# Retention into a routed mixture of experts: small gate loads on another queue, and the first pair's loads and transposes reordered

## The chip, the core and the metric

The kernel runs on one core of a Trainium2 chip. The metric is the device time of one execution in microseconds (us), the median of several runs. A core has five engines that matter here. TensorE (PE, with its weight loads shown as PEld) multiplies and transposes. VectorE (DVE) and ScalarE (ACT) copy and combine. GpSimd (POOL) does elementwise work, scatters rows, and starts some transfers. SyncE (SP) starts nearly all transfers. "SPq" or "ACTq" in a row is the time in which an engine issues a transfer.

## The reference

```python
for t in range(S):                       # retention; B=4, H=8, S=768, D=64
    state = gamma * state + outer(k[:, :, t], v[:, :, t])
    y[:, :, t] = scale * einsum('bhd,bhde->bhe', q[:, :, t], state)
x = y.transpose(0, 2, 1, 3).reshape(3072, 512)
logits = x @ w_gate                      # 8 experts
e_idx = argmax(logits, axis=1)
gate_w = softmax(logits)[arange, e_idx]
eom = sigmoid(x @ w_output_gate)
for e in range(8):                       # w1: 8 x 512 x 1024, w2: 8 x 1024 x 512
    ye = relu(x[e_idx == e] @ w1[e]) @ w2[e]
    out[e_idx == e] = gate_w * eom[:, e] * ye
```

All data are float32.

## The kernel before

The retention is done in chunks of 128 tokens: six chunks for each of four batch rows, 24 in all. Two batch rows run side by side, so that the chunks come in 12 pairs. The loop over pairs (variable `p`, lines 686 to 828) is written out by hand in the order in which each engine is to work; nothing is reordered afterwards. Chunk numbers `n0 = 2p` and `n1 = 2p + 1` are the two of a pair.

For one pair the steps on TensorE are, in this order: the part that comes from the running state (`inter`, L385), the products of keys and queries (`scores`, L393, into four PSUM banks `sp[0]` to `sp[3]`, chunk `n0` in banks 0 and 1), the transposes of finished tokens of an earlier pair (`tokens`, L522), of gate logits (`turn_logits`, L448) and of queries for a later pair (`turn_queries`, L353), then the products with the values (`values`, L411), the state's update (`state`, L418), the counts for the router, the transposes of the next pair's keys (`turn_keys`, L340), more queries, and the gate logits (`logits`, L437). VectorE masks the scores (L401), scales the outputs (L428) and does the routing. ScalarE copies every transposed tile from PSUM to SBUF: keys and queries by the helper of L336, tokens as rows by L529 in `rows_out`. GpSimd scales the values (`prep_v`, L330), writes the row numbers into each row (L531) and scatters rows by expert into a DRAM table, `srt` (L538). A bank of `sp` can be written again only when its last reader is done, so a copy of ScalarE can hold TensorE up.

Queries are loaded for two chunks at a time (`load_q`, 512 KB, two buffers). For the very first tiles each batch row has a buffer of the same two, `q0`, loaded and turned in halves: `first_queries(ch, o)` (L303) loads half `o`, and `turn_first` (L358) and `keep_first` transpose and copy it. Half 0 serves pair 0, half 1 serves pair 1. `load_q(0, 1)` and `load_q(1, 1)` go into the buffers of `q0` and so wait for both halves to be turned. Pair 1 turns these queries: `part_queries` on ScalarE copies them apart into `qr` (by L336), and `turn_queries` transposes them, row 0's between the scores and the values of pair 1, row 1's near its end. From pair 2 to pair 9 one batch row's queries for a later pair are turned in each pair (`ahead`).

Loads of keys and values go through SP in program order: keys have six buffers, values four. Each transfer from SP or ACT signals on one of eight counters, handed out in turn. A transfer that reuses a counter waits for the one that had it before; the listings below show these waits as `DMAHW0` to `DMAHW7`.

The gate tables `w_gate` and `w_output_gate` are loaded into `wg` by four transfers of 8 KB (L314), which the first `logits` needs, at the end of pair 0. GpSimd starts the loads of the decay tables `gn` and `ga`. Before the first transposes TensorE runs nine products with zeros (`warm_up`).

At the loop's end a first part of one expert is computed from rows read back from `srt` (`head_load`, L573, issued in pair 10 when all scatters so far have landed). Then eight experts follow, with nearly nothing but matmuls (L985, L1008).

Of the kernel before, what the change touches and what calls it, by code (L numbers as in the profile page):

```python
# [33 lines left out]
def retention_moe_kernel(  # L34
# [14 lines left out]
    nc = tc.nc  # L49
    P = 128  # L50
    HP = P // 2
    B, H, S, D = q.shape
    E, DM, DF = w1.shape
    NT = B * S
    NC = S // P
    NCH = B * NC
# [181 lines left out]
    with ExitStack() as actx:  # L238
# [14 lines left out]
        def rows(x):  # L253
            return slice(x * HP, x * HP + HP)
# [56 lines left out]
        nc.scalar.dma_start(gv, dec_v)  # L311
        for o in range(2):
            for x, w in ((0, w_gate), (E, w_ogate)):
                nc.scalar.dma_start(wg[rows(o), :, x:x + E],  # L314
                                    w[o * DM // 2:(o + 1) * DM // 2].rearrange("(g p) e -> p g e", p=HP))
        load_v(0)
# [6 lines left out]
        load_v(3)  # L323
        load_q(0, 1)
        load_q(1, 1)

# [5 lines left out]
        def blocks(bank):  # L332
            return bank.rearrange("p (g t) -> p g t", g=NG)
# [184 lines left out]

        def tokens(i):
            px = blocks(sp[i % 2])  # L520
            for g in range(NG):
                nc.tensor.transpose(px[:, g], yts[i][:, g], ident)  # L522
            pxs[i] = px
# [142 lines left out]
        for o in range(2):  # L666
# [3 lines left out]
                            dec_c.rearrange("b x -> (b x)").unsqueeze(0).broadcast_to([P, 2 * NC * NG]))  # L670
        warm_up(misc, 9)
        turn_first(0, 0, yp[0])
        keep_first(0, 0, yp[0], nc.vector)
        turn_keys(0, yp[1])
        keep_keys(0, yp[1])
        turn_first(1, 0, st.rearrange("p a x -> p (a x)"))
        keep_first(1, 0, st.rearrange("p a x -> p (a x)"), nc.vector)
# [8 lines left out]
        for p in range(NCH // 2):  # L686
# [6 lines left out]

            if n0 + 4 < NCH:
                load_k(n0 + 4)
                load_v(n0 + 4)
            if p > 0 and nxt // 2 + 1 < NQ:
                load_q(nxt % 2, nxt // 2 + 1)
            if n1 + 4 < NCH:
                load_k(n1 + 4)  # L700
                load_v(n1 + 4)
# [13 lines left out]

            if p == 0:
                for ch in range(2):
                    turn_first(ch, 1, sp[ch])
                    keep_first(ch, 1, sp[ch], nc.scalar)
            if p >= 2:  # L720
                for i in (n0 - 4, n0 - 3):
                    tokens(i)
                    rows_out(i)
                    if not last:
                        scatter(i)
            if grp:
                turn_logits(grp)
            if p == PICK_AT:
                by = rank_key(totals(n0), io8)
# [4 lines left out]
            if p == 1:  # L734
# [3 lines left out]
                for r in range(2):  # L738
                    part_queries(1, 1, r)
            if ahead:  # L740
                turn_queries(*ahead, 0, sp[0])
                keep_queries(*ahead, 0, sp[0])
            if p == 10:
# [30 lines left out]
            if grp:  # L774
                bank = sp[3 if last else 0]
                counts(grp, bank)
                add_counts(grp, nc.gpsimd)
                route2(grp, bank)
                gates(grp, bank[:, 6 * E:6 * E + 4])
            if n0 + 2 < NCH:  # L780
                turn_keys(n0 + 2, sp[2])
                keep_keys(n0 + 2, sp[2])
                turn_keys(n0 + 3, sp[3])
                keep_keys(n0 + 3, sp[3])
# [7 lines left out]
            if last:  # L792
                for i in (n0 - 2, n0 - 1):
                    tokens(i)
                run_head(12)
                rows_out(n0 - 2)
                scatter(n0 - 2)
# [50 lines left out]
        for i in grp:  # L848
            tokens(i)
            rows_out(i)  # L850
            scatter(i)
            run_head(6)
# [406 lines left out]
```

## Time and profile before

| | |
|---|---|
| median of 3 runs | 421.1 us (419.83 to 422.4) |
| the profiled execution | 421.54 us |
| its span, first to last instruction | 419.6 us |
| TensorE busy | 404.4 us, 96% of the span |
| GpSimd, VectorE, ScalarE busy | 257.3, 222.8, 185.3 us |
| mean granted TensorE clock | 0.987 of full speed |
| moved by DMA | 75.75 MB, mean 181 GB/s |

The profile shows one execution. A row of its timeline has a start, a duration, an engine, a line of the kernel, an operation with its output and input, and a count; square brackets give the idle time of that engine just before and what ended it. Matmul ends are modelled, so that a busy TensorE isn't always one at its peak. The chain is followed back from the last instruction: at each step to what released it.

### The profile page before, as it was taken

The numbers are of one execution on the slowest core, as the hardware profiler recorded it, in microseconds if no ns is written. First come the engines' busy times: TensorE is split into PE (matmuls) and PEld (weight loads), VectorE is DVE, ScalarE is ACT, GpSimd is POOL, SyncE is SP. The second block draws the span as 40 slices with busy tenths as digits, with TensorE's granted clock in tenths as the row PEclk, the third lists the DMA queues.
The fourth block names the chain that finished last, engine by engine and source line by source line (L and its number), as shares of the span: only waits on it lengthen the run. The fifth ranks groups of instructions, "written<-read, shape, count | busy, mean of one in ns | idle before, by whom it ended". The sixth has DMA issues, their size and how long they took to land.

```text
span 419.6 us, 10492 instructions
## 1 busy us (share of the span) xinstructions
PE 404.4 (96%) x3611; PEld 378.3 (90%) x3611; DVE 222.8 (53%) x557; ACT 185.3 (44%) x360; POOL 257.3 (61%) x306
## 2 busy tenths in 40 slices
PE   7999999999999999999999999999999999999990
PEld 4878887888879999999999999999999999999880
DVE  3355667666687766744543553563555454553120
ACT  2366555555565325634533544443454454452110
POOL 3655664454587127883367777777786787876702
PEclk9899999999999999999999999999999999999996
DMA  8999788988744969797494588469459659620102
GB/s 187 256 240 244 214 232 220 252 204 220 203 141 154 248 147 269 222 211 191 141 224 140 148 200 207 155 180 232 136 172 237 176 168 208 214 75 28 47 3 75
DMA packets 130157, 75.75 MB, mean 181 GB/s; under 512 B 61748, under 2 KB 118216, under 8 KB 130064
## 3 DMA queue, kind: packets, MB, share of 16 engines
q1 hardware_dynamic: 122928, 59.38, 58.1%
q0 software_dynamic: 5904, 15.04, 10.3%
q8 instruction: 61, 1.00, 1.0%
q14 instruction: 32, 0.26, 0.2%
q10 hardware_dynamic: 1232, 0.06, 0.2%
HBM read 59.71 MB, written 15.30 MB: 179 GB/s over the span
## 4 chain that ended last, share of the span: by engine, by line
PE 79%; issue 5%; POOL 5%; DMA 5%; DVE 2%; ACT 1%; SPq 1%; POOLq 0%; ACTq 0%; DVEq 0%
PE h L985 29%; PE a L1008 27%; PE y L411 4%; PE s L393 4%; PE s L353 2%; PE st L418 2%; PE y L385 2%; POOL out_dram L215 2%; PE s L340 2%; PE s L522 1%; DMA qn<-in_q_dram 1%; PE s L622 1%; PE a L1036 1%; DMA raw<-in_moe_w_dram 1%; DMA srt<-row,pos 1%
## 5 line engine op out<-in xcount | busy, mean ns | idle before, releaser
L201 POOL TENSOR_TENSOR wlo<-raw,whi 128x512 fp32r<-128x512 f32 x56 | 74.9, 1338 | 44.3 <-ACT whi L193 27.1
L215 POOL DMA_INDIRECT out_dram<-ot,idi x85 | 84.7, 996 | 22.5 <-issue 17.7
L985 PE MATMUL h<-xh,whi 128*128 128x360 f32 (+5 forms) x256 | 84.3, 329 | 0.1
L985 PE MATMUL h<-xw,whi 128*128 128x360 f32 (+5 forms) x256 | 84.3, 329 | 0.0
L985 PE MATMUL h<-xh,wlo 128*128 128x360 f32 (+5 forms) x256 | 84.2, 329 | 0.0
L995 DVE SCALAR_TENSOR_TENSOR hl<-h,hh 128x192 fp32r<-128x192 f32 (+7 forms) x64 | 35.4, 554 | 82.8 <-ACT hh L994 81.2
L1008 PE MATMUL a<-hh,whi 128*128 128x392 f32 (+4 forms) x224 | 73.8, 329 | 0.0
L1008 PE MATMUL a<-hl,whi 128*128 128x392 f32 (+4 forms) x224 | 73.8, 329 | 0.0
L1008 PE MATMUL a<-hh,wlo 128*128 128x392 f32 (+4 forms) x224 | 73.5, 328 | 0.0
L994 ACT ACTIVATE hh<-h 128x192 fp32r<-128x192 f32 (+7 forms) x64 | 31.2, 488 | 73.5 <-PE h L985 73.5
L192 ACT CAST whi<-raw 128x512 fp32r<-128x512 f32 x64 | 39.6, 618 | 40.9 <-PE a L1008 31.1
L200 DVE TENSOR_TENSOR wlo<-raw,whi 128x512 fp32r<-128x512 f32 x60 | 42.4, 707 | 27.2 <-ACT whi L192 22.9
L985 PEld LDWEIGHTS h<-xh,whi 128*128 128x128 f32 x256 | 48.2, 188 | 0.9 <-issue 0.4
L985 PEld LDWEIGHTS h<-xw,whi 128*128 128x128 f32 x256 | 48.2, 188 | 0.6
L985 PEld LDWEIGHTS h<-xh,wlo 128*128 128x128 f32 x256 | 48.2, 188 | 0.2
L538 POOL DMA_INDIRECT srt<-row,pos x24 | 24.2, 1007 | 38.9 <-ACT row L529 31.2
L401 DVE TENSOR_TENSOR am<-s,mask 128x512 f32<-128x512 f32 x48 | 29.9, 684 | 30.6 <-PE s L393 28.5
L1008 PEld LDWEIGHTS a<-hl,whi 128*128 128x128 f32 x224 | 42.2, 188 | 0.3
L1008 PEld LDWEIGHTS a<-hh,wlo 128*128 128x128 f32 x224 | 42.2, 188 | 0.2
L1008 PEld LDWEIGHTS a<-hh,whi 128*128 128x128 f32 x224 | 42.2, 188 | 0.2
L193 ACT CAST whi<-raw 128x512 fp32r<-128x512 f32 x64 | 39.6, 618 | 1.1 <-DMA raw<-in_moe_w_dram 1.1
L927 ACT CAST xh<-xt 128x416 fp32r<-128x416 f32 (+2 forms) x28 | 15.1, 540 | 36.7 <-DVE xt L926 36.7
(201 smaller groups left out, 642.1 us busy)
## 6 DMA issues: line engine op xcount, KB each, us to landing
raw<-in_moe_w_dram SPq DMA_DIRECT2D x128, 128.0 KB, 4.8
raw<-in_moe_w_dram SPq DMA_DIRECT2D x64, 256.0 KB, 4.1
kn<-in_k_dram SPq DMA_DIRECT2D x24, 256.0 KB, 4.6
vn<-in_v_dram SPq DMA_DIRECT2D x24, 256.0 KB, 5.0
qn<-in_q_dram SPq DMA_DIRECT2D x10, 512.0 KB, 5.6
xl<-srt SPq DMA_DIRECT2D x12, 209.6 KB, 5.5
xl<-srt SPq DMA_DIRECT2D x8, 225.8 KB, 3.3
xl<-srt SPq DMA_DIRECT2D x8, 193.5 KB, 4.8
```

What stands on the lines that cost most here:

```text
L192: nc.scalar.copy(hi[:, 0], raw[:, 0])
L193: nc.scalar.copy(perm(hi), r2)
L200: (first or nc.vector).tensor_sub(lo[:, 0], raw[:, 0], hi[:, 0].bitcast(F32))
L201: (second or nc.gpsimd).tensor_sub(perm(lo), r2, perm(hi).bitcast(F32))
L215: st = nc.gpsimd.indirect_dma_start(out=dst, out_offset=bass.IndirectOffsetOnAxis(ap=idx, axis=0), in_=src, in_offset=None, bounds_check=n ...
L393: nc.tensor.matmul(sp[2 * (n % 2) + b][:, (2 * S_ + o) * P:(2 * S_ + o) * P + P], kt[n][rows(b), g], queries(n, g, b), start=True, stop=Tr ...
L401: nc.vector.tensor_tensor(out=a.rearrange("p s o t -> p (s o) t"), in0=sp[2 * (n % 2) + b].rearrange("p (x t) -> p x t", t=P), in1=mask.un ...
L538: s_ = nc.gpsimd.indirect_dma_start(out=srt, out_offset=bass.IndirectOffsetOnAxis(ap=rt.pop(("pos", i)), axis=0), in_=row.rearrange("p a x ...
L985: nc.tensor.matmul(ps[:, 0:C], l[:, 0, w], r[:, dc, 0:C], start=(n == 0), stop=(n == 3 * NDC - 1))
L994: nc.scalar.activation(hh, ps[:, 0:C], AF.Relu)
L995: nc.vector.scalar_tensor_tensor(out=hl, in0=ps[:, 0:C], scalar=0.0, in1=hh.bitcast(F32), op0=ALU.max, op1=ALU.subtract)
L1008: nc.tensor.matmul(accs[d][:, 0:C], l[:, 1, w], r[:, 0:C], start=(f == 0 and n == 0), stop=(f == NF - 1 and n == 2))
```

## The change

- The four loads of the gate tables move from ACT's queue to GpSimd's, behind `gn` and `ga`.
- Of the nine zero products seven stay ahead of the first transposes, and three come behind the first keys' transposes.
- The loads of row 0's and row 1's second queries (`load_q(0, 1)`, `load_q(1, 1)`) move into pair 0, each behind one of the loads of keys 4 and 5; the loads of values 4 and 5 come behind all of these.
- The second halves of the first queries are turned at the end of pair 0, behind the state's update, and not between its scores and values. Row 1's copy goes from ScalarE to VectorE.
- From pair 2 on the queries are turned first behind the scores, in bank 0; then the tokens of chunk `n0 - 4` in bank 1, the logits, and the tokens of chunk `n0 - 3` in bank 0. Both scatters come behind both `rows_out`.

```diff
-        for o in range(2):
-            for x, w in ((0, w_gate), (E, w_ogate)):
-                nc.scalar.dma_start(wg[rows(o), :, x:x + E], ...
...
-        load_q(0, 1)
-        load_q(1, 1)
...
-        def tokens(i):
-            px = blocks(sp[i % 2])
+        def tokens(i, bank):
+            px = blocks(bank)
...
-        warm_up(misc, 9)
+        for o in range(2):
+            for x, w in ((0, w_gate), (E, w_ogate)):
+                nc.gpsimd.dma_start(wg[rows(o), :, x:x + E], ...
+        warm_up(misc, 7)
         turn_first(0, 0, yp[0])
         keep_first(0, 0, yp[0], nc.vector)
         turn_keys(0, yp[1])
         keep_keys(0, yp[1])
+        warm_up(misc, 3)
         turn_first(1, 0, st.rearrange("p a x -> p (a x)"))
...
-            if n0 + 4 < NCH:
+            if p == 0:
+                load_k(n0 + 4)
+                load_q(0, 1)
+                load_k(n1 + 4)
+                load_q(1, 1)
+                load_v(n0 + 4)
+                load_v(n1 + 4)
+            elif n0 + 4 < NCH:
...
-            if p == 0:
-                for ch in range(2):
-                    turn_first(ch, 1, sp[ch])
-                    keep_first(ch, 1, sp[ch], nc.scalar)
+            if ahead:
+                turn_queries(*ahead, 0, sp[0])
+                keep_queries(*ahead, 0, sp[0])
             if p >= 2:
-                for i in (n0 - 4, n0 - 3):
-                    tokens(i)
-                    rows_out(i)
-                    if not last:
-                        scatter(i)
+                tokens(n0 - 4, sp[1])
+                rows_out(n0 - 4)
             if grp:
                 turn_logits(grp)
+            if p >= 2:
+                tokens(n0 - 3, sp[0])
+                rows_out(n0 - 3)
+                if not last:
+                    scatter(n0 - 4)
+                    scatter(n0 - 3)
...
-            if ahead:
-                turn_queries(*ahead, 0, sp[0])
-                keep_queries(*ahead, 0, sp[0])
...
+            if p == 0:
+                for ch in range(2):
+                    turn_first(ch, 1, sp[ch])
+                    keep_first(ch, 1, sp[ch], nc.vector if ch else nc.scalar)
             if n0 + 2 < NCH:
                 turn_keys(n0 + 2, sp[2])
```

First, SP's queue at the kernel's start, from its fourth transfer on (`kn` keys, `vn` values, `qn` queries; L303 loads a half of the first queries, L274 a whole tile; in brackets the engine or counter waited for). Before:

```order
L264 DMA kn<-in_k_dram 128x8x64 [waits DMAHW0_49]
L269 DMA vn<-in_v_dram 128x8x64 [waits DMAHW1_49]
L269 DMA vn<-in_v_dram 128x8x64 [waits DMAHW2_49]
L303 DMA qn<-in_q_dram 64x16x64 [waits DMAHW3_49]
L303 DMA qn<-in_q_dram 64x16x64 [waits DMAHW4_49]
L264 DMA kn<-in_k_dram 128x8x64 [waits DMAHW5_49]
L264 DMA kn<-in_k_dram 128x8x64 [waits DMAHW6_49]
L269 DMA vn<-in_v_dram 128x8x64 [waits DMAHW7_49]
L269 DMA vn<-in_v_dram 128x8x64 [waits DMAHW0_49]
L274 DMA qn<-in_q_dram 128x8x128 [waits DMAHW3_49,DMAHW1_49,PE_49]
L274 DMA qn<-in_q_dram 128x8x128 [waits DMAHW4_49,DMAHW2_49,PE_49]
L264 DMA kn<-in_k_dram 128x8x64
```

And now:

```order
L264 DMA kn<-in_k_dram 128x8x64
L269 DMA vn<-in_v_dram 128x8x64 x2
L303 DMA qn<-in_q_dram 64x16x64
L303 DMA qn<-in_q_dram 64x16x64 [waits DMAHW0_49]
L264 DMA kn<-in_k_dram 128x8x64 [waits DMAHW1_49]
L264 DMA kn<-in_k_dram 128x8x64 [waits DMAHW2_49]
L269 DMA vn<-in_v_dram 128x8x64 [waits DMAHW3_49]
L269 DMA vn<-in_v_dram 128x8x64 [waits DMAHW4_49]
L264 DMA kn<-in_k_dram 128x8x64 [waits DMAHW5_49]
L274 DMA qn<-in_q_dram 128x8x128 [waits DMAHW7_49,DMAHW6_49,PE_49]
L264 DMA kn<-in_k_dram 128x8x64
L274 DMA qn<-in_q_dram 128x8x128 [waits DMAHW0_49,PE_49]
```

Four early transfers have lost their wait for a counter, and the two large query loads stand one and two key loads later, still waiting for TensorE.

Second, TensorE in pair 0, from the last scores (`qt`, `kt` are turned queries and keys) to the next pair's keys. Before:

```order
L393 MATMUL s_127<-qt,kt 128x128
L358 MATMUL s_124<-ident,qn 128x64 x8
L358 MATMUL s_125<-ident,qn 128x64 x8
L411 MATMUL y_129<-am_246,vs 64x128 x4
L411 MATMUL y_130<-am_248,vs 64x128 x4
L411 MATMUL y_129<-am_258,vs 64x128 x4
L411 MATMUL y_130<-am_260,vs 64x128 x4
L418 MATMUL st<-vs,kn 64x64 x16
L340 MATMUL s_126<-ident,kn 128x128 x4
L340 MATMUL s_127<-ident,kn 128x128 x4
```

And now, with the lines of the changed file:

```order
L387 MATMUL s_127<-qt,kt 128x128
L405 MATMUL y_129<-am_247,vs 64x128 x4
L405 MATMUL y_130<-am_249,vs 64x128 x4
L405 MATMUL y_129<-am_259,vs 64x128 x4
L405 MATMUL y_130<-am_261,vs 64x128 x4
L412 MATMUL st<-vs,kn 64x64 x16
L352 MATMUL s_124<-ident,qn 128x64 x8
L352 MATMUL s_125<-ident,qn 128x64 x8
L334 MATMUL s_126<-ident,kn 128x128 x4
L334 MATMUL s_127<-ident,kn 128x128 x4
```

The sixteen half-query transposes moved from ahead of the values to behind the state's update.

Third, TensorE in pair 3, between scores and values (`s_124` and `s_125` are banks 0 and 1, `yt` tokens, `lt` logits, `qr` queries). Before:

```order
L393 MATMUL s_127<-qt,kt 128x128
L522 MATMUL s_124<-ident,yt 128x128 x4
L522 MATMUL s_125<-ident,yt 128x128 x4
L448 MATMUL misc<-ident,lt 128x128 x2
L353 MATMUL s_124<-ident,qr 128x128 x4
L411 MATMUL y_129<-am_733,vs 64x128 x4
```

And now:

```order
L387 MATMUL s_127<-qt,kt 128x128
L347 MATMUL s_124<-ident,qr 128x128 x4
L516 MATMUL s_125<-ident,yt 128x128 x4
L442 MATMUL misc<-ident,lt 128x128 x2
L516 MATMUL s_124<-ident,yt 128x128 x4
L405 MATMUL y_129<-am_734,vs 64x128 x4
```

The queries went from last to first, and the second use of bank 0 is now by tokens.

## Rows read from the trace of the kernel before

**Rows 1.** The page's chain that ended last, shares of the span.

```profile
PE 79%; issue 5%; POOL 5%; DMA 5%; DVE 2%; ACT 1%; SPq 1%; POOLq 0%; ACTq 0%; DVEq 0%
```

**Rows 2.** The chain, first 34 us: start, duration in us, what.

```profile
2.29 6.12 DMA qn<-in_q_dram
...
9.87 3.52 PE s L393 x32
...
14.24 0.68 PE s L358 x8
14.91 1.90 PE y L411 x32
...
20.37 1.99 PE s L393 x32
...
22.72 0.90 PE s L353 x8
...
33.01 1.10 PE s L522 x7
```

**Rows 3.** TensorE by windows: stretch, length, busy, granted clock, DMA share, GB/s.

```profile
5.00:9.20 4.20, 2.62 (x22) 1.00 1.21 240
9.20:12.60 3.40, 3.40 (x30) 0.55 1.11 244
```

**Rows 4.** Timeline of the first 35 us.

```profile
1.25 4.02 PE L167 MATMUL misc<-wz 128*128 128x512 bf16 x9 [1.25 <-DVE warm L90]
...
3.27 0.61 POOL L669 DMA_DIRECT2D ga<-in_dec_c_dram  x1
4.73 0.39 SPq L264 DMA_DIRECT2D kn<-in_k_dram  x1
8.45 0.71 PE L358 MATMUL st<-ident,qn 64*128 64x64 f32 x8 [1.58 <-DMA qn<-in_q_dram]
9.91 2.04 POOL L330 TENSOR_TENSOR vs<-vn,gv 128x512 f32<-128x512 f32 x2 [6.03 <-DMA vn<-in_v_dram]
14.65 2.23 SPq L274 DMA_DIRECT2D qn<-in_q_dram  x2
20.47 1.14 ACT L336 COPY qr<-qn 128x512 f32<-128x512 f32 x2 [0.70 <-DMA qn<-in_q_dram]
...
31.12 1.14 ACT L336 COPY qr<-qn 128x512 f32<-128x512 f32 x2 [0.69 <-DMA qn<-in_q_dram]
```

**Rows 5.** DMA from 2 to 30 us, all queues.

```profile
DMA packets 23585, 6.76 MB, mean 241 GB/s; under 512 B 20485, under 2 KB 23519, under 8 KB 23583
```

**Rows 6.** DMA from 2 to 8.4 us, ACT's queue: packets, MB, share.

```profile
q10 hardware_dynamic: 1232, 0.06, 12.1%
```

**Rows 7.** Timeline of pair 5, scores to values.

```profile
62.30 2.48 DVE L401 TENSOR_TENSOR am<-s,mask 128x512 f32<-128x512 f32 x4 [2.69 <-PE s L393]
...
63.09 1.21 PE L522 MATMUL s<-ident,yt 128*128 128x128 f32 x8
63.84 1.28 ACT L529 ACTIVATE row<-s,gate 128x512 f32<-128x512 f32 x2 [2.17 <-PE s L522]
...
64.59 0.42 PEld L353 LDWEIGHTS s<-ident,qr 128*128 128x128 f32 x4 [0.31 <-ACT row L529]
...
65.32 1.02 POOL L538 DMA_INDIRECT srt<-row,pos  x1 [3.69 <-ACT row L529]
...
66.82 0.98 POOL L538 DMA_INDIRECT srt<-row,pos  x1 [0.28 <-POOL row L531]
```

**Rows 8.** Waits from 30 to 125 us: total, times, longest.

```profile
PEld s L353 <- ACT row L529: 1.8, 6, 0.4
...
PEld y L411 <- POOL vs L330: 0.8, 1, 0.8
```

**Rows 9.** The chain in pairs 9 to 11.

```profile
105.51 4.82 DMA srt<-row,pos
...
116.52 1.03 POOL srt L538
```

More of the change, by code (lines that the diff above doesn't have):

```diff
@@ L311, in retention_moe_kernel @@
         nc.scalar.dma_start(gv, dec_v)
-        for o in range(2):
-            for x, w in ((0, w_gate), (E, w_ogate)):
-                nc.scalar.dma_start(wg[rows(o), :, x:x + E],
-                                    w[o * DM // 2:(o + 1) * DM // 2].rearrange("(g p) e -> p g e", p=HP))
         load_v(0)
@@ L670, in retention_moe_kernel @@
                             dec_c.rearrange("b x -> (b x)").unsqueeze(0).broadcast_to([P, 2 * NC * NG]))
-        warm_up(misc, 9)
+        for o in range(2):
+            for x, w in ((0, w_gate), (E, w_ogate)):
+                nc.gpsimd.dma_start(wg[rows(o), :, x:x + E],
+                                    w[o * DM // 2:(o + 1) * DM // 2].rearrange("(g p) e -> p g e", p=HP))
+        warm_up(misc, 7)
         turn_first(0, 0, yp[0])
@@ L692, in retention_moe_kernel @@
             last = p == NCH // 2 - 1
-            if n0 + 4 < NCH:
+            if p == 0:
[6 more added lines that the diff above has]
+            elif n0 + 4 < NCH:
                 load_k(n0 + 4)
                 load_v(n0 + 4)
-            if p > 0 and nxt // 2 + 1 < NQ:
-                load_q(nxt % 2, nxt // 2 + 1)
-            if n1 + 4 < NCH:
+                if nxt // 2 + 1 < NQ:
+                    load_q(nxt % 2, nxt // 2 + 1)
                 load_k(n1 + 4)
@@ L793, in retention_moe_kernel @@
                 for i in (n0 - 2, n0 - 1):
-                    tokens(i)
+                    tokens(i, sp[i % 2])
                 run_head(12)
@@ L848, in retention_moe_kernel @@
         for i in grp:
-            tokens(i)
+            tokens(i, sp[i % 2])
             rows_out(i)
```

## The prediction

> **What bounds the kernel now.** I read the chain of waits first, then the clock by windows, the timeline of the first 35 us, and the timeline of one middle pair. TensorE holds 79% of the chain [rows 1], and from the second half on it is nothing but matmuls that the change doesn't touch. What the change can move lies in the first 125 us: the start, where the chain goes through a load, and the waits between scores and values.
>
> At the start the chain is one load: the first half of row 1's queries, issued at 2.29 and landed at 8.41 [rows 2]. TensorE stands idle for 1.58 us until then [rows 4]. After that gap the granted clock falls: it is 1.00 from 5.0 to 9.2 and 0.55 from 9.2 to 12.6 [rows 3], that is mostly the lower level (1.2 GHz), in a stretch in which TensorE is busy throughout. The 32 score products of pair 0 take 3.52 us there, those of pair 1 take 1.99 [rows 2]. DMA is the second bound: 6.76 MB go from 2 to 30 us, 241 GB/s in the mean [rows 5], and twice ScalarE waits for queries of a later pair (at 20.47 and 31.12 [rows 4]).
>
> In a middle pair TensorE hardly waits. The one wait that the change aims at is 0.31 us, where the queries' transposes need bank 0 and ScalarE is still copying tokens out of it [rows 7]; all of these come to 1.8 us from 30 to 125 us [rows 8].
>
> **The change part by part, the start.** The gate loads: ACT's queue used 12.1% of the DMA engines from 2 to 8.4 us, 0.77 us [rows 6]. The four gate loads are 4 x 256 of its 1232 packets, so 0.64 us. GpSimd can begin them at 3.88 (3.27 + 0.61 [rows 4]), so part of them still goes ahead of row 1's queries. Bounds: 0 and 0.64 us earlier; I take 0.3.
>
> The Trainium skill, "DMA: Bandwidth & Descriptors", section "Issuing engines are not separate DMA queues", says that transfers started by ScalarE, SyncE or GpSimd run on the same 16 engines and interleave, so that another starter saves only the time of issuing. By it the 0.3 would be 0. No row here shows gate loads that GpSimd issues.
>
> GpSimd pays for them with its own time. The trace has no such issue on GpSimd; the nearest rows are 0.61 us for `ga` [rows 4] and 1.02 for a scatter [rows 7]. Four end between 6.3 and 8.0. GpSimd then waits for the values anyway, until 9.91 [rows 4], so I count nothing. The cover is gone from 1.5 us each on ((9.91 - 3.88) / 4).
>
> SP's earlier transfers: the fourth was held until 4.73 [rows 4], and is now free at once. The engines were at 240 GB/s from 5.0 to 9.2 [rows 3], against a mean of 241 [rows 5], so an earlier issue mostly lengthens the queue. I count it only as what keeps DMA from running dry.
>
> The zero products: nine took 4.02 us, 0.45 each [rows 4]. Seven free TensorE 0.9 us earlier, but the next thing it needs, row 1's queries, isn't there earlier by that. The three behind the first keys last up to 1.34 us and lie in the idle 1.58, so they cost nothing unless the queries land over 0.24 us earlier than now; at full clock they are shorter. They leave at most about 1.0 us of idle time where 1.58 stood. Whether the clock then holds isn't in any row. Bounds: 0 and 1.53 us (3.52 - 1.99); I take it that it holds, as TensorE's time between 5 and 9.2 is filled much better than before.
>
> Pair 0 by my choices: scores start at 9.57 and end at 11.56. VectorE masks bank by bank at 0.62 each (2.48 / 4 [rows 7]), from 10.6 to 13.15. The values' scaling is done at 11.95 (9.91 + 2.04 [rows 4]). The last quarter of the value products comes behind the last mask, a quarter of 1.90, and ends at 13.65, where it was 16.81 (14.91 + 1.90 [rows 2]). So 3.16 us are gained, but the half-query transposes, twice 0.68 [rows 2], which lay beside the masks, now stand by themselves behind the state: 1.8 left. They also put one more copy of ScalarE (0.57, half of 1.14 [rows 4]) ahead of the key copies. I take 0.3 us of that as visible: 1.5.
>
> What is late next is the load of row 0's second queries. It waits for both halves to be turned, it stands behind keys 4, and pair 1's query transposes at 22.72 [rows 2] need it. Before, it was issued at 14.65, landed at 20.47 [rows 4], and had 1.7 us of slack with a copy of 0.57. Keys 4 ahead of it cost 0.262 MB / 241 GB/s = 1.1 us. It can make up at most that by DMA that never runs dry. So it lands between 20.4 and 21.6, and the transposes come at 21.0 to 22.2: a gain of 0.5 to 1.7 us, whatever TensorE gained. A second cap stands behind: the next queries land at 31.12 [rows 4], with nothing removed ahead of them, are copied by 31.7, and are now wanted right behind pair 2's scores, where the tokens stood at 33.01 [rows 2]: 1.3 us. I take 1.1 for the whole start.
>
> **The change part by part, pairs 2 to 11.** In eight pairs the queries go first. TensorE's work between the two uses of bank 0 is the same: four transposes in between and the logits. The copy that has to be done in time is now that of the queries, 0.57, and no more that of the tokens, 0.64 (1.28 / 2 [rows 7]). So of each 0.31 us wait about 0.06 goes: 0.5 us in all. Bounds: 0, and the whole 1.8 plus pair 2.
>
> The first scatter of a pair comes 0.84 us behind the first tokens' copy (63.84 + 0.64, 65.32 [rows 7]). That copy is now 0.58 later, behind the queries'. Between the two scatters lay 0.48 us (65.32 + 1.02 to 66.82, of which 0.28 idle [rows 7]), 0.20 of it a copy that goes ahead. So the second ends 0.4 later. That hides in GpSimd's wait of 3.69 [rows 7], except in pair 9: there the chain runs through that scatter's landing [rows 9] into the read of sorted rows, and 0.4 us count. Pair 10's scatters, also on the chain [rows 9], get 0.2 back. In pairs 10 and 11 no queries are turned, and the tokens go first into bank 1, whose mask ends 0.62 later than bank 0's: nearly 0.5 us twice, against the 0.8 us in which TensorE waited for GpSimd there [rows 8] and the 0.5 gained before. It hides. Sum: -0.5 + 0.4 - 0.2 = -0.3.
>
> **Sum.** 1.1 + 0.3 = 1.4 us off. The profiled execution, 421.54 us with a span of 419.6, becomes 420.1; it lies 0.44 above the median, and on the median of 421.1 the same gives 419.7.
>
> **The rivals.**
> - Scores stay cold. For: nothing shows how little idle time the clock forgives, and seven zero products instead of nine open a new gap ahead of the first transposes. Then pair 0's scores take 3.52 from 9.57, masks end near 14.4, values at 14.9, and with 1.36 for the moved transposes and 0.3 for copies 0.25 us is left: 0.25 + 0.3 = 0.55 off, 420.5.
> - DMA doesn't bind. For: 241 GB/s is a mean with stretches in which SP was held. Then row 1's queries land 0.64 earlier, the start gains 1.5 + 0.3, and pairs 2 to 9 lose half of their waits, 0.9: 2.7 off, 418.4. Against: both caps.
> - Slower: the second queries come late. Their load now waits for transposes behind the state, not behind the scores. If the scores stay cold these end near 16.5, where they ended at 14.92 (14.24 + 0.68 [rows 2]), so the issue at 14.65 becomes 16.5 or more. With 5.8 us to landing and 1.1 for keys 4 they land at 22.3 to 23.4 and pair 1 stalls; row 1's, one key load further back, then hold ScalarE, which has pair 1's state to copy. It decides once they land after 22.15 (22.72 - 0.57), and costs 0.7 to 2.9 us: less 0.3, about 422.6.
> - GpSimd late. At twice a scatter's 1.02 us each, the four issues would end at 12.0, the values' scaling 2.1 us late, pair 0 about 1.5 worse than forecast: 421.2.
>
> The trace has GpSimd's issue of `ga` at 0.61 us [rows 4]. The Trainium skill, "SBUF — State Buffer", section "SBUF: two separate sides", warns that GpSimd can't write the descriptors of its transfers while VectorE runs certain operations, so that one which takes about 620 ns alone (section "A bandwidth-pool intuition that's wrong") takes about 3100. The trace agrees with the lower figure, and nothing here shows the higher; by that the four would end near 16.3, an estimate, and GpSimd would be late.
>
> **How the numbers follow.** Forecast 0.47, cold scores 0.22, DMA not binding 0.14, late queries 0.12, GpSimd late 0.05. The likeliest case alone spans 418.9 to 420.6. For 8 in 10 I go from 418.0, which holds most of the third case, to 422.3, half of the fourth. A change of 0.5%, 2.1 us, is about what a measurement of this kernel can tell from none: faster is below 419.0, slower above 423.2. Faster: most of the third case and a quarter of the forecast, 0.26. Slower: half of the late queries and the tail of GpSimd, 0.08. The rest, 0.66.
>
> **What would show it.** Right: a granted clock near 1.00 from 9 to 13 us, pair 0's scores in about 2 us, values ending near 13.7, pair 1's query transposes at 21 to 22 us with ScalarE waiting for the load just before, a 0.25 us wait in each middle pair, now ahead of tokens, and the first scatter 0.6 later within its pair. Wrong: scores at 3.5 us (cold), query copies landing after 22 us, GpSimd's value scaling starting later than 10 us, or a middle pair more than 0.2 us shorter, which would mean that the reordering is worth more than one copy's difference.

## The result: slower, by a stop in code that wasn't touched and by a longer end

The changed kernel takes 423.22 us (median of 22 runs, 421.0 to 427.53), the kernel before 420.48 on the same chip (22 runs, 419.42 to 424.0): ratio 1.0056, 95% interval 1.0038 to 1.0074. The ratio is that of the fast runs, without the one of 427.53 us. The forecast was 419.7 with a range up to 422.3. The profiled execution took 423.69 us, its span is 421.8.

Up to the main loop the profiled execution gains 0.44 us, where 1.4 was forecast. The chain of the kernel after, first 24 us (start, duration, what):

```profile
3.25 6.12 DMA kn<-in_k_dram
...
10.13 1.99 PE s L387 x32
...
13.35 1.16 PE y L405 x16
14.51 0.93 PE st L412 x32
...
16.24 5.37 DMA qn<-in_q_dram
...
21.62 0.63 ACT qr L330
...
22.30 1.18 PE s L347 x8
```

The scores take 1.99 us in place of 3.52 [rows 2], and the clock holds, where it was 0.55 [rows 3]. A window with no record of the clock reads 1.00; the record begins at 4.75 us here and at 6.11 in the kernel before, so the 1.00 of [rows 3] is a reading from 6.11 on only.

```profile
5.00:9.20 4.20, 2.27 (x21) 1.48 (x19) 0.69 (x1) 0.59 (x1) 1.34 (x3) 1.00 1.12 233
9.20:12.60 3.40, 3.17 (x46) 2.73 (x44) 1.97 (x4) 0.59 (x1) 2.19 (x3) 1.00 1.06 236
```

TensorE was busy for 2.27 us of the first window, less than before (2.62 [rows 3]). What it waited for next came no earlier: row 1's first queries let it go on at 8.61 (8.45 [rows 4]), the scores begin at 10.13 (9.87 [rows 2]), and the values' scaling begins at 10.39 (9.91 [rows 4]).

The next limit is the late load of the second queries: ScalarE waits for it, 3.02 us idle, where it waited 0.70 [rows 4]. GpSimd issues the gate tables in 0.65 us each and is then held by the load of the values, not by its own work:

```profile
3.85 0.65 POOL L667 DMA_DIRECT2D wg<-in_moe_w_gate_dram  x1
...
8.61 0.71 PE L352 MATMUL st<-ident,qn 64*128 64x64 f32 x8 [1.74 <-DMA qn<-in_q_dram]
...
10.39 2.05 POOL L324 TENSOR_TENSOR vs<-vn,gv 128x512 f32<-128x512 f32 x2 [4.05 <-DMA vn<-in_v_dram]
...
21.62 1.14 ACT L330 COPY qr<-qn 128x512 f32<-128x512 f32 x2 [3.02 <-DMA qn<-in_q_dram]
```

In the pairs the wait on bank 0 is smaller and has moved to the tokens (1.8 us before [rows 8]). The second row is the wait on bank 1 in pairs 10 and 11; the 0.8 us for GpSimd [rows 8] are gone. Waits from 30 to 125 us:

```profile
PEld s L516 <- ACT qt L330: 1.4, 8, 0.3
...
PEld s L516 <- DVE am L395: 1.3, 2, 0.7
```

In pair 5 the first scatter starts 3.56 us behind the first mask, where it was 3.02 (65.32 - 62.30 [rows 7]): 0.5 later, as forecast 0.6.

```profile
61.92 2.48 DVE L395 TENSOR_TENSOR am<-s,mask 128x512 f32<-128x512 f32 x4 [2.69 <-PE s L387]
...
65.48 1.03 POOL L532 DMA_INDIRECT srt<-row,pos  x1 [4.09 <-ACT row L523]
```

The loss lies behind all this. Stretches of the two profiled executions, in us, from the starts of the first matmul of each rank (ranks are the experts in the order of their size):

| stretch | before | after | |
|---|---|---|---|
| up to the main loop | 151.97 | 151.53 | -0.44 |
| ranks 1 to 4 | 125.93 | 125.88 | -0.05 |
| rank 5 | 34.06 | 35.46 | **+1.40** |
| ranks 6 to 8, to the last matmul's start | 97.39 | 97.18 | -0.21 |
| from there to the last scatter's start | 1.76 | 1.75 | -0.01 |
| last scatter's start to the end of the span | 8.47 | 10.03 | **+1.56** |

Rank 5 holds a stop in the middle of twelve matmuls that follow one another without a semaphore. The chain of the kernel after:

```profile
279.70 2.11 PE a L1016 x12
281.81 1.43 PE h L993 x8
283.23 1.27 issue
284.50 0.98 PE h L993 x4
```

"Issue" means that nothing in the profile held the engine. The instruction queues suggest what did, and the experiments below bear it out. The page of the kernel after:

```profile
q8 instruction: 61, 1.00, 1.0%
q14 instruction: 33, 0.27, 0.2%
```

Queue 8 brings 61 pieces of 16,384 bytes, queue 14 brings 33 of 8,192, while the kernel runs. Queue 8 is taken to be TensorE's program and queue 14 that of the other engines; the profile doesn't name them. A count of the built program, which no profile shows, puts the weight load ahead of the ninth matmul at instruction 8190 of TensorE, with 64 B each two short of the edge at 8192. The trace has the fetch of the next piece from 281.94 to 282.98, and the ninth matmul at 284.50, 2.56 us behind the fetch's start. So the stop is a sum: the fetch starts 0.29 us behind the step's first matmul, the code is usable 2.56 later, and eight matmuls of 0.178 us pass meanwhile: 0.29 + 2.56 - 1.42 = 1.43 late. (Of that the chain calls 1.27 "issue".) The kernel before has the same edge five matmuls later in its program (10 instructions: one warm-up product of two, eight added waits), its fetch starts at 282.04, and its matmuls are late by 0.14 only, from the 13th on (284.41).

The Trainium skill, "Advanced Engine Details and Errata", section "ISA Cache", says that a line of an engine's instruction memory is 16 KB, or 256 instructions. The trace agrees for the 61 pieces of queue 8 and not for the 33 of queue 14, which are of 8 KB. What a late line costs, the 2.56 us here, that section doesn't say.

The end is GpSimd's closing sequence, which the profile doesn't count as busy. From the packed trace, GpSimd alone (start and duration in us; `before_pool7` is explained below):

```
before          after           before_pool7
411.11 0.98     411.80 0.98      409.81 0.98   last scatter
413.34 0.02     414.87 0.02      412.42 0.02   wait
413.43 0.02     416.99 0.02      412.51 0.02   wait
  ... 3 more      ... 3 more       ... 3 more
414.31 0.04     417.35 0.04      413.18 0.04   wait
415.91 0.69     417.44 0.83      413.27 0.69   INC_SWDGE_SEM
416.63 2.12     418.30 2.69      414.00 2.12   DRAIN
```

Both kernels stand still once in it, before for 1.6 us ahead of the seventh instruction, after for 2.1 us ahead of the second. Counted from the beginning of GpSimd's program it is the same place, number 1043: the gate tables put five instructions more in front. Queue 14 starts a piece at 413.57 in the kernel before and at 414.37 in the kernel after, 2.34 and 2.62 us ahead of the end of the stop, much as on TensorE; in all 13 profiles with this stop it is 2.1 to 2.6. That the stop waits for this piece is argued: the profile doesn't name the engine, a piece starts then in the seven profiles without the stop too, and 1043 isn't a multiple of the 128 instructions that 8 KB would hold at 64 bytes. The drain is 0.57 us longer.

### The profile page after: what moved, and what is told of

Same layout as the page of the kernel before. It is cut to its first block, busy times and chain, and to the rows that moved or that the text cites. A ratio compares the mean times of both kernels' runs of the same rounds, so it can differ in the third digit from the quotient of the medians.

```text
span 421.8 us, 10498 instructions
## 1 busy us (share of the span) xinstructions
PE 402.2 (95%) x3612; PEld 375.9 (89%) x3612; DVE 223.9 (53%) x558; ACT 185.5 (44%) x359; POOL 260.0 (62%) x310
## 4 chain that ended last, share of the span: by engine, by line
PE 87%; issue 4%; DMA 3%; POOL 2%; DVE 1%; SPq 1%; ACT 0%; DVEq 0%; POOLq 0%
PE h L993 29%; PE a L1016 27%; PE y L405 5%; PE s L387 5%; PE s L516 3%; PE s L616 3%; PE y L596 2%; PE s L347 2%; PE y L379 2%; PE st L412 2%; PE s L334 2%; POOL out_dram L215 2%; DMA kn<-in_k_dram 1%; PE misc L431 1%; PE a L1044 1%
## 5 line engine op out<-in xcount | busy, mean ns | idle before, releaser
L201 POOL TENSOR_TENSOR wlo<-raw,whi 128x512 fp32r<-128x512 f32 x56 | 75.0, 1340 | 45.5 <-ACT whi L193 31.4
L1002 ACT ACTIVATE hh<-h 128x192 fp32r<-128x192 f32 (+7 forms) x64 | 31.3, 489 | 73.8 <-PE h L993 73.8
```

Of the source, the lines that this page charges most:

```text
L201: (second or nc.gpsimd).tensor_sub(perm(lo), r2, perm(hi).bitcast(F32))
L1002: nc.scalar.activation(hh, ps[:, 0:C], AF.Relu)
```

## The experiments

Theory A: what counts is where the code lies against the edges of its pieces, and how soon their fetch starts. Theory B: chance of one execution, or transfers that meet. Others are named where they came up. The runs were made on different chips. On two of them (the runs marked 430) the kernel before takes about 430 us, on the others 420 to 421; ratios are always to the kernel before on the same chip.

**TensorE's code.** First the changed kernel again:

> The changed kernel as it is, a second profile of it. Theory A (where the code lies): the main loop again starts near 151.7 us on TensorE (152.14 in the kernel before), TensorE again stands still 1.2 to 1.3 us in front of the ninth of twelve matmuls of the second step of expert rank 5, and from the last scatter's start to the span's end it is again about 10.0 us, so about 2.5 us over the kernel before. Theory B (accident of one execution, or transfers that meet): the stop is gone or stands at another place, the end is nearer 8.5 us, and the span nearer 419.5 us.

Measured (430): 437.78, ratio 1.0153 (1.0102 to 1.0203). The stop is there at the same matmul with the same 1.27 us, the end 9.5 us. As A had it, and not as B. But the main loop starts at 161.3 us, which neither had said (below).

The kernel before, its code moved by 10:

```diff
-        warm_up(misc, 9)
+        warm_up(misc, 8)
+        for _ in range(6):
+            nc.tensor.matmul(misc[:, 0:85], wz[:, 0:P], wz[:, 0:85], start=True, stop=True)
```

> The kernel before, with the last of its nine 512-column warm-up matmuls cut into six of 85 columns: five weight loads and five matmuls more, nearly the same columns, nothing else. TensorE's program behind them lies 10 instructions further on, as it does in the changed kernel. Theory A (where the code lies): the 1.27 us stop of the changed kernel appears here, before the ninth matmul of the second step of rank 5; span and time go up by 1.2 to 1.5 us, the end of the program (8.5 us from the last scatter) stays. Theory B (accident, or transfers that meet): no stop, within 0.3 us of the kernel before. Theory C (one of the three parts of the change itself costs it, through queue or semaphores): no stop either, since none of the three is in.

Measured (430): 1.0013 (0.9984 to 1.0041). A miss in size: the ninth matmul is late by 0.34 us, not by 1.4, and the time alone doesn't tell A from B or C. Its fetch started 1.05 us ahead of the step, in the changed kernel 0.29 behind the step's start; from fetch to use it is 2.81 and 2.56. So the place alone doesn't set the stop. It sets how much time the fetch has, and the fetch's start varies.

The changed kernel, its code moved by 246 more:

```diff
+        def pad(s, n, C):       # only in the arm for the largest size, which isn't taken
+            ...
+                nc.tensor.matmul(hps[s % 4][:, 0:C], hi[:, 0, 0:P], xs[e][0][:, 0, 0:C], ...)
...
+                if e == 1:
+                    first_mm.insert(0, lambda C: pad(s, 18 if f < 5 else 17, C))
```

> The changed kernel with 123 matmuls (246 instructions) in arms of the second expert rank's steps that the data don't take, so they are never executed; from rank 3 on TensorE's program lies 256 instructions behind where it lies in the kernel before, that is at the same place within a 16 KB piece (10 + 246 = 256 instructions of 64 B: the program's 15,018 were fetched in 61 pieces, 1.00 MB). Theory A (where the code lies): no stop in rank 5, the main loop 1.3 us shorter, span near 420.5 us, about 1.3 us under the changed kernel; the end of the program stays near 10 us, since GpSimd's program hasn't moved. Theories B and C: as the changed kernel within 0.3 us. Either could lose up to 2 us more where the longer unused arms are jumped over.

Measured (430): the stop is gone (late by 0.37), rank 5 takes 34.29 us, 1.17 less than in `after_again`. The time, 438.15, is no lower, where 1.3 us less was expected. The six runs of either kernel lie over 2 and 9 us apart, so their medians can't show it; the profiled execution, the longest of its six, also started its main loop 1.2 us later.

And moved by 8 the wrong way:

```diff
-        warm_up(misc, 7)
+        warm_up(misc, 6)
+        for _ in range(5):
+            nc.tensor.matmul(misc[:, 0:102], wz[:, 0:P], wz[:, 0:102], start=True, stop=True)
```

> The changed kernel with one of its first seven warm-up matmuls cut into five (8 instructions more, the same columns): the 16 KB edge in rank 5's second step falls before the fifth of its twelve matmuls in place of the ninth. Theory A: the stop stands there, 0.7 us longer than in the changed kernel if the fetch starts as early: 1.6 to 2.1 us; time 0.5 to 0.9 us over the changed kernel (1.004 to 1.0056 of the kernel before), so about 1.006 to 1.007. Theory B: the stop stays where and as long as it was, or goes.

Measured: 425.16, ratio 1.0098 (1.0068 to 1.0127). The stop is where A put it and 1.95 us long; the time is more than forecast, and the granted clock then falls to the lower level (0.51 for 3.4 us), which costs 1.04 us more. Chain and windows:

```profile
281.10 0.72 PE h L995 x4
281.81 1.95 issue
283.76 2.23 PE h L995 x8
285.99 3.15 PE a L1018 x12
```

```profile
281.00:284.60 3.60, 1.65 (x10) 1.33 (x9) 1.80 (x4) 1.14 (x2) 2.16 (x2) 1.00 1.12 195
284.60:288.00 3.40, 3.40 (x12) 3.40 (x11) 0.58 (x1) 0.51 (x1) 1.45 (x2) 0.51 1.18 226
288.00:292.00 4.00, 4.00 (x24) 4.00 (x24) 0.78 (x2) 1.65 (x3) 1.51 (x2) 0.99 0.62 153
```

The twelve second products take 3.15 us in place of 2.11. All profiles together, by the matmul of the step that the trace shows late (late: its start less the start of the one before, less 0.18; a step has twelve first and twelve second products):

| late matmul | late, us | kernels |
|---|---|---|
| 5 | 2.11 | after_pe8 |
| 9 | 1.43, 1.43, 1.15, 0.89, 0.89, 0.34 | after, after_again, after_gates_back, after_third, after_pool2, before_pe10 |
| 10 | 0.71 | only_mid |
| 13 | 0.56, 0.40, 0.28, 0.14, 0.14 | only_start_2, only_gates, only_start, before, before_2 |
| none | 0 | before_pool7 |
| 13 or 14, code moved by 256 | 0.14 to 0.43 (six) | after_pe256, after_both (2), realigned (2), mid_realigned |

**GpSimd's code and the gate tables.**

```diff
-            nc.gpsimd.iota(rows, ...)
+            for _ in range(3):          # in the overflow part, never executed
+                nc.gpsimd.iota(rows, ...)
```

> The changed kernel with two GpSimd instructions (one iota written three times) in the part that runs only when tokens overflow, which they don't here: never executed. GpSimd's closing instructions lie two further on, so that all of them begin behind the place at which both kernels waited for code (before its seventh closing instruction in the kernel before, before its second in the changed one: the same place in the program, counted from its beginning). Theory A: that wait, 2.1 us between the first two closing instructions of the changed kernel, goes, and the end comes 1.5 to 2 us earlier: 8 to 8.5 us from the last scatter; the 1.27 us stop of TensorE stays; time 1.5 to 2 us under the changed kernel. Theories B and C: the end stays near 10 us or moves without an order to it.

Measured (430): 7.95 us from the last scatter to the end, 1.6 less than in `after_again`; as A had it. The median, 437.14 against 437.78, is 0.64 lower and not 1.5 to 2, and with six runs each that shows nothing either way.

The gate tables alone on GpSimd, and the changed kernel with them back:

```diff
-                nc.scalar.dma_start(wg[rows(o), :, x:x + E], ...     # only_gates; after_gates_back
+                nc.gpsimd.dma_start(wg[rows(o), :, x:x + E], ...     # is the reverse on the kernel after
```

> The kernel before with the first part of the change alone: the four gate-table loads issued by GpSimd and no longer by ScalarE. GpSimd's program lies 5 instructions further on, TensorE's one. Theory E (the gate tables on GpSimd's queue are paid for at the end: GpSimd's closing drain took 2.69 us in all of the kernels with them there and 2.12 us in all without, and its closing instructions wait once more for code): from the last scatter to the end 9.5 to 10 us in place of 8.5, everything before it as in the kernel before; 1.0 to 1.5 us slower. Theory A alone (only where the code lies): 0.7 to 1 us slower, with the drain at 2.12 us. Theory F (the new start of the first pair is what costs most runs about 3 us, through the clock or the late query loads): as the kernel before within 0.5 us.

> The changed kernel with the four gate-table loads back on ScalarE's queue, in their old place. GpSimd's program lies where it lies in the kernel before; TensorE's 9 instructions further on. Theory E: closing drain 2.12 us, 8.5 us from the last scatter to the end, 1.2 to 1.5 us faster than the changed kernel; what is left over the kernel before is the stop of up to 1.4 us in rank 5 (theory A). Theory F: no faster than the changed kernel in the median, since the start is left as it is, though drain and end go back.

Measured: 1.0036 (1.0013 to 1.0058) and 1.0022 (0.9996 to 1.0048); ends of 9.52 and 8.42 us, drains of 2.69 and 2.12. Then the unchanged kernel with eight of those `iota` in place of one:

> The kernel before with seven GpSimd instructions in the overflow part that never run: its closing instructions lie just where they lie in the changed kernel with two more, which ended 7.8 to 8.0 us after the last scatter with a drain of 2.69 us. Theory A: 7.2 to 7.5 us from the last scatter to the end, drain 2.12 us; about 1.1 us faster than the kernel before. Theory E alone (the end depends on the gate tables, not on where the code lies): 8.4 to 8.7 us, as the kernel before.

Measured: 419.68, ratio 0.9971 (0.9947 to 0.9994), end 7.14 us; the listing above shows the 1.6 us wait gone. All profiles:

| closing code | gate tables by | profiles | end, us | drain |
|---|---|---|---|---|
| as before | ScalarE | 5 | 8.42 to 8.71 | 2.12 |
| 5 on | GpSimd | 8 | 9.52 to 10.03 | 2.69 |
| 7 on | GpSimd | 3 | 7.84 to 7.95 | 2.69 |
| 7 on | ScalarE | 4 | 7.02 to 7.23 | 2.12 |

So the place of the code is worth 1.3 to 1.8 us, and the gate tables, at one place, 0.75 (7.9 less 7.15), 0.57 of it the drain. Both A and E have a share. In the mean of each row the kernels with GpSimd's gate loads end 1.19 us later than those like the kernel before (9.69, 8.50), so 1.56 is a large draw.

**The start and the pairs.**

> The changed kernel once more, to stand beside the three runs that go with it. Theory A (where the code lies against the 16 KB and 8 KB pieces in which it is fetched, and how soon the fetch starts): the stop before the ninth matmul of rank 5's second step is there with 0.7 to 1.3 us, the end of the program takes 9.5 to 10 us from the last scatter. Theory D (TensorE's instructions come slower on some chips): where the kernel before takes about 430 us, TensorE also stands still, short of instructions, twice a pair in the state matmuls, 0.4 to 0.7 us each, and starts the main loop near 161 us; where the kernel before takes about 420 us, it doesn't, and the main loop starts near 151.7.

Measured: 422.73 (1.0040, 1.0018 to 1.0061), stop 0.73 us, end 9.75. The start is another one. No clock is recorded before 13.7 us, and the durations are those of the lower level (1.2 GHz) throughout, although the windows up to there read 1.00: the first pair's scores take 3.38 us again, and the second pair's start at 20.96, not at 19.1. The chain of `after_third`:

```profile
10.79 3.38 PE s L387 x32
14.17 2.10 PE y L405 x32
...
20.96 1.99 PE s L387 x32
```

> The kernel before with the third part of the change alone: from the second pair on the query transposes stand ahead of the token transposes, and both use other banks. TensorE's program lies 8 instructions further on than in the kernel before (all eight are waits), GpSimd's not at all. Theory A: main loop start 0 to 0.3 us earlier, a stop of 0.5 to 1.1 us in rank 5, the end as before (8.5 us); in all 0.3 to 1 us slower. Theory D on a chip of the 430 us kind: the added wait in each pair is what costs the state matmuls their second stop, so nearly all of the loss before the main loop is here, +3 to +5 us; on a chip of the 420 us kind nothing of it. Theory B (no part costs anything, the rest is chance): same as before within 0.3 us.

> The changed kernel without its third part: gate tables on GpSimd's queue, first pair's loads in the order of use, its second query halves turned late, ten warm-up matmuls in two lots. TensorE's program lies 2 instructions further on than in the kernel before, GpSimd's 5. Theory A: the start of the main loop 0.2 to 0.5 us earlier than before, no stop over 0.3 us in rank 5, the end near 10 us: 1 us slower than before in all. Theory D on a chip of the 430 us kind: the state matmuls' stops as in the kernel before, one a pair, main loop within 0.5 us of the kernel before. Theory B: 0.3 to 0.5 us faster than before.

Measured: `only_mid` (kernel before, the lines from `turn_queries` to the second scatter as in the change) 1.0031 (1.0003 to 1.0059), `only_start` (kernel after, those lines as before) 1.0069 (1.0046 to 1.0092). From the third pair's scores to the last pair's `only_mid` takes 87.36 us, the kernel before 87.83: the third part gains 0.5 there and loses 0.7 in rank 5. For `only_start` about 1 us was expected and 2.9 measured; its profile is of 420.83 us, the lowest of its five runs. A second profile of it, and one of the kernel before:

> The changed kernel without its third part, again: its profile was of a run of 420.83 us, while the other four took 423.2 to 424.2. Theory F (two kinds of start): a run of the slow kind shows the first pair's scores at the low clock (3.3 us in place of 1.8) and the second pair's scores at 20.9 in place of 19.0 us, and the 1.9 us are still there at the main loop. Theory G (what differs lies behind the attention): the start is of the same kind or has been made up for by the main loop, and 2 to 3 us are lost in the main loop or at the end (a stop of TensorE in the last rank, a longer end).

> The kernel before, for a second profile beside the others of this chip. Theory A: no stop over 0.3 us in rank 5, 8.4 to 8.7 us from the last scatter to the end, drain 2.12 us, first pair's scores at the low clock (3.3 us), second pair's at 20.3 to 20.9 us, main loop start 152 to 153 us. Theory B (chance alone makes the stops): a stop of TensorE here too, somewhere.

Measured: 1.0056 (1.0030 to 1.0082) and 0.9986 (0.9969 to 1.0004). Main loop starts of 150.67 and 150.64 us: the new start had nothing left at that point. The kernel before again has no stop and an end of 8.44. The 2.8 us between the two spans lie behind: 0.65 in rank 5, 0.85 in ranks 6 to 8, 1.23 at the end. Then both places of code moved:

> The changed kernel with both lots of instructions that are never executed: 246 in unused arms of rank 2's steps on TensorE, two on GpSimd in the overflow part. Theory A: no stop over 0.3 us in rank 5, the end 8 us or less from the last scatter; 2 to 3 us under the changed kernel of the same chip, so on a chip of the 420 us kind 0.3 to 1 us faster than the kernel before. Theory B: as the changed kernel. Theory D says nothing here: what TensorE loses before the main loop on a chip of the 430 us kind stays.

> The changed kernel with 246 and two instructions never executed, a second profile. Theory A+E: the end 7.8 to 8.0 us, no stop over 0.3 us in rank 5, median 0.3 to 0.7 us over the kernel before less what the start gives, that is within 0.2% of it. Theory F (start of two kinds): a slow run shows the second pair's scores at 20.9 us in place of 19.1 and keeps that. Theory G: a slow run has its 3 us in the main loop or the end, at a place not seen so far.

Measured: first 1.0051 (1.0025 to 1.0076), a miss, as it should have been 0.3 to 1 us faster than the kernel before; its profile, of the lowest time (420.26), has no stop and an end of 7.84. Then 0.9999 (0.9978 to 1.0020). The second profile, of the highest time (422.57), shows the third kind of start: the clock holds as in the kernel after, then TensorE waits for the second queries, and the clock falls in pair 1. Chain and window:

```profile
17.98 4.96 DMA qn<-in_q_dram
22.97 0.63 ACT qr L330
23.64 1.18 PE s L347 x8
24.82 3.25 PE y L405 x32
```

```profile
23.60:28.00 4.40, 4.36 (x44) 4.09 (x46) 1.77 (x7) 2.84 (x6) 0.26 (x2) 0.68 0.96 235
```

The value products take 3.25 us in place of 1.90, and the third pair's scores start at 33.64, where the kernel after had 30.66. So a loss of about 3 us in the start, as F has it for `only_gates`, is there in this run, but not by F's sign: the second pair's scores start at 19.40, not 20.9. Over all profiles the third pair's scores start at 29.9 to 33.6 us with the new start (13, mean 31.4), at 30.7 to 32.0 with the old one (7, mean 31.3).

**Both costs taken away.** The kernel after with the gate tables back, `pad`, and eight `iota`:

> The changed kernel with the gate tables back on ScalarE's queue, 246 instructions never executed in TensorE's arms of rank 2 and seven never executed on GpSimd in the overflow part. Theory A+E (place of the code, and the drain that the gate tables lengthen): rank 5 at 34.1 to 34.3 us without a stop over 0.3 us, drain 2.12 us, 7.3 us from the last scatter to the end (8.4 less the wait for code, 1.1), so with the start's 0.3 us the kernel is 1.0 to 1.5 us faster than the kernel before, ratio 0.9965 to 0.998. If the two were not the whole loss: within 0.3% of the kernel before, or over it.

Measured: 419.33, ratio 0.9963 (0.9935 to 0.9990), end 7.17 us, 0.26 us of stop in rank 5. The time is as A and E forecast, and the lowest of the study. But `before_pool7`, the kernel before with one line changed, comes within the interval (419.68): beside it the change, its two costs taken away, is worth 0.35 us in the median and nothing that these runs can tell. The code's new place isn't free either. The profile, of the highest time (423.08), has another stop, in rank 6:

```profile
330.51 0.71 issue
```

It ends 2.97 us behind the start of a fetch on queue 8 (328.25). Ranks 6 to 8 take 98.03 us there, in the other profiles of the 420 chips 96.48 to 97.71; neither that stop nor this spread is explained.

> The kernel before with the third part of the change alone (query transposes ahead of the token transposes), 248 instructions never executed in TensorE's arms of rank 2 and seven on GpSimd in the overflow part, so that neither stop is there. Theory H (the new start gives nothing on the mean): 1.3 to 1.6 us faster than the kernel before, 0.4 us from the pairs and 1.1 from the end, as fast as realigned or faster; ratio 0.996 to 0.997. Theory of the prediction (the start gives 1.1 us): 1.1 us slower than realigned.

> The changed kernel with the gate tables back on ScalarE's queue and the code moved, again, beside mid_realigned on the same chip. Theory H: within 0.4 us of mid_realigned in the median, with a wider spread. Theory of the prediction: 1.1 us faster than mid_realigned.

Measured (430): 433.44 and 433.08, ratios 1.0109 (1.0078 to 1.0139) and 1.0096 (1.0068 to 1.0124). The two lie 0.36 us apart in the median and 0.65 in the mean; with six runs each that is good to about 0.75 (my estimate from their spread), so it doesn't tell H's 0 to 0.4 from the prediction's 1.1. Against H's 1.3 to 1.6 us faster, `mid_realigned` is 4.1 slower than the kernel before on that chip: a miss, which the last section takes up.

## Why the prediction was wrong

- The step that failed is in its first paragraph: "from the second half on it is nothing but matmuls that the change doesn't touch". From that I took that nothing behind 125 us can change, and put the place of the code at nothing. The change adds ten instructions to TensorE's program and five to GpSimd's, and all code behind them lies elsewhere. In the profile shown that cost 1.40 us in rank 5, and about 0.8 of the 1.56 at the end (less the 0.75 of the next point). Moving the code moved, lengthened or removed both.
- "So I count nothing" for GpSimd's four issues was right at the start (0.65 us each, cover not used up; the values' scaling does start later than the 10 us named as a sign, at 10.39, but it waits for the values' load) and wrong at the end: 0.75 us at the same place of the code.
- The start, 1.1 us, came to 0.29 in the profile shown (third pair's scores at 30.66, before 30.95; pair 0's values end at 14.51 and not 13.7). The order of events was right there: the clock held, and the second queries were next. Two of its terms were not. The gate loads were to bring row 1's queries 0.3 us earlier; they came 0.16 later (8.61 against 8.45), and the scores began at 10.13, not 9.57. And the clock was to hold because TensorE's time from 5 to 9.2 us is filled better; it was filled less (2.27 us of 4.20 against 2.62), with a last gap of 1.74 us where 1.58 stood. So that it held is luck by the reason given, and what decided it the rows don't show.
- That it holds was also taken as given for every execution. With seven warm-up products (one of them cut up in `after_pe8`) the record of the clock begins, at the higher level, by 5 us in four of 13 profiles, by about 10 us in two, and from 13 us on in seven. With nine (one cut up in `before_pe10`) it begins by 7 us in all seven, and the clock falls again between 7.7 and 10.1. Where it did hold, the second queries took most of the gain back, or more. On the mean the term is nothing: 31.4 against 31.3 us at the third pair's scores.
- That is the first rival (cold scores) in half of the profiles and the third (second queries late) in one: `after_both_2` is 2.7 us behind the kernel before at the third pair (33.64 less 30.95), 1.35 of it value products at the lower clock, which the rival didn't have. Its price of 0.7 to 2.9 us doesn't follow from its own landing times, which lie 0.15 to 1.25 us past 22.15. That its 422.6 is near the measured 423.2 is luck: in the profile shown the loss lies elsewhere. I had the rivals as exclusive cases of the whole kernel; they are kinds of one execution.
- The pairs, 0.3 us, were right on the chips where the kernel before takes 420 to 421 us: 0.1 in the kernel after (87.73 against 87.83), 0.3 in `after_gates_back` and `realigned`, 0.5 in `only_mid`.

## What to carry to other kernels

An edit that adds or drops a few instructions early moves all code behind it. So compare the stretches that the edit doesn't touch as well: a stop put down to "issue" in straight code, and the time from the last transfer's start to the end of the span, can tell of fetching. Before an idea worth less than 1% is judged, put the code back to its old place, with instructions in an arm that isn't taken, and see whether the new place has a stop of its own, as `realigned` has. And of a clock that hangs on a gap early in a kernel one profile shows one draw.

## What the runs showed of the hardware that I had not expected

- A piece of TensorE's code is usable 2.3 to 2.8 us after its fetch starts, and the fetch starts between 1.05 us before and 0.42 us after the step that jumped there, from execution to execution. The jump itself is decided 1.76 to 1.85 us ahead of the step in all 20 profiles. After a stop of 1.95 us the clock fell to 0.51 for 3.4 us; after one of 1.27 it didn't.
- On the 430 chips the new order of the transposes costs 3.6 to 4.1 us in the pairs. TensorE stands still in the state's products, with nothing shown to wait for. From 40 to 125 us, in `before_pe10`, `after_again` and `mid_realigned` in turn:

```profile
PEld st L418 <- issue: 2.1, 5, 0.5
```

```profile
PEld st L412 <- issue: 4.7, 11, 0.6
```

```profile
PEld st L418 <- issue: 5.8, 14, 0.5
```

The same pairs take 93.3, 97.4 and 96.9 us there. Of the change `mid_realigned` has only the third part, and its unexecuted code lies behind the pairs, so it is that part's doing: theory D as put for `only_mid`. The only profile there without the third part is `before_pe10`, on another chip than `mid_realigned`. The profiles of the other chips have no such row. The third part adds one wait to TensorE's stream in each of eight pairs; that this wait is the cause is only argued, and wasn't tried.
- The pairs aren't all that is lost on the 430 chips. In all six profiles of them, and in none of the others, TensorE waits 2.2 to 2.8 us near 405 to 411 us for ScalarE's copy of the last expert's first products, and in four of the six the clock is then at the lower level for 3.4 us. From 403 to 425 us in `after_again`:

```profile
ACT hh L1002 <- remote: 9.5, 1, 9.5
...
PE a L1044 <- ACT hh L1002: 2.8, 1, 2.8
```

"Remote" means that the profile names no instruction of this core; what holds ScalarE is open.
- Left open: why six of eight runs of `after_both` took 422 to 424.3 us and its second lot 419.6 to 422.6. The third kind of start accounts for 3 us, but none of those six runs has a profile.
